# Retention with a snake feed-forward layer on one core: three q loads and two k loads by rows of eight tokens, decay tables by doubling on GpSimd, and another order of the first token group

## The chip, the cores and the metric

The kernel runs on one core of one Trainium2 chip. The metric is the device time of one execution in microseconds (us), the median of several runs. A core has TensorE (PE in the profile; PEld is its weight load), VectorE (DVE), ScalarE (ACT), GpSimd (POOL) and SyncE (SP), and 16 DMA engines.

## The reference, cut to what matters

```python
def _attn_ref(q, k, v):                      # q, k, v: (4, 8, 768, 64), float32
    gamma = 1.0 - 2.0 ** (-5.0 - np.arange(H))
    for t in range(S):
        state = gamma[None, :, None, None] * state + einsum('bhd,bhe->bhde', k[:, :, t], v[:, :, t])
        y[:, :, t] = D ** -0.5 * einsum('bhd,bhde->bhe', q[:, :, t], state)

def _moe_ref(x, w_in, w_out, alpha):         # x: (3072, 512), w_in: (512, 2048), w_out: (2048, 512)
    h = x @ w_in
    s = np.sin(alpha * h)
    return (h + s * s / (alpha + 1e-09)) @ w_out

x = attn.transpose(0, 2, 1, 3).reshape(B * S, H * D);  out = _moe_ref(x, ...)
```

Four sequences go through a retention layer with a decay gamma of its own for each of 8 heads; its result, per token the 8 heads side by side, goes through two matrix products with a snake function between them. The output is float32.

## The kernel before, in words

Each sequence of 768 tokens is cut into 6 chunks of 128 tokens, 24 in all. The list `order` puts the first chunk of each of the four sequences first (e0 to e3), then the other five of each; P[n] below is its n-th chunk. `sizes` makes ten groups of 4, 2, 2, 2, 2, 2, 2, 2, 2 and 4 chunks. A group passes the feed-forward layer together: a `Slot` takes one or more of 16 slices f of 128 hidden features. Its matmuls (L481) make `ph` in PSUM, ACT takes the sine (L484), ACT or DVE squares it (`sq("A")`, L489, or `sq("D")`, L491), and DVE's `add` (L496) writes `gT`. `ff_out` (L506) multiplies a slice of `gT` by `w_out` into `po`, for one chunk at a time. While a group's slots run, the `ff_out` of the group before fills TensorE between them, and the retention of the chunks of the next group is put in by a table (`where`, `atts`).

Retention of the first chunks needs no state: `half_T` transposes q (i=0) and k (i=1) on TensorE by an identity, `stage_A` (L276) makes the scores and has DVE multiply them by the decay matrix `dec` (L286), `stage_M` (L306) multiplies by v, and ACT copies the result to `xT`. For later chunks `burst` does it all: `inter` (q by the state `s_q`), `round_of` or `mix` (masked scores by v), `scores` of the next chunk, `sums` or `round_of` (k by v, for the state). A `nop` that waits for an earlier matmul (`behind`) stands in each burst. There the decay is taken by powers: v is scaled by `kg` or `kgq` (`scale_v`), the result by `qg[:, c]`, the table for chunk c of a sequence (`leave`, L433). `first_state` makes the state after e0; that after e1, e2 and e3 is made in the burst that ends the sequence before, from the raw k and v of those chunks.

Loads are issued on GpSimd, which casts float32 to bfloat16 on the way, one by one in the order of the program. A chunk load (`load_chunk`, L100) puts 128 tokens on 128 partitions, so its pieces are one head of one token: 1024 pieces of 256 B read and 128 B written for 128 KB. A half of a quarter of `w_in` (L131) is 512 pieces of 512 B written, a quarter of `w_out` (L135) 512 pieces of 1024 B, half of it 256. Only q and k of e0 come through SP, in float32 (`near`), and are cast on chip. The next 16 loads stand at the top; the other early ones are issued behind the front part of the program.

Ahead of the first feed-forward slot TensorE is kept busy with `idle_work(n)`: n matmuls of 512 columns on zeros. The tables for decay are made there too: `dec` by ACT from `tio` (the token index along the row), then multiplied by the mask on DVE (L563); `qg[:, 0]` by four Exps on ACT (`grow`, L554); `step` by five small Exps; `qg[:, c]` for c above 0 by one multiplication on GpSimd each (L229). `tok` is written by two iotas on GpSimd (L165). An Exp table and later a Sin table are loaded on ACT (L178, L588).

Group 0 (e0 to e3) is written out by hand (L657 to L708). Slices 0 to 3 are first computed for three chunks only (384 columns), while e3 is still on its way; then e3's 128 columns of the four slices in one Slot (`nf=4`, 16 matmuls), then slices 4 to 15 with 512 columns each. `F(ts, fs)` runs `ff_out` for several chunks. P[4], P[5] and P[6] are transposed (`stage_T`, L264) and the first two bursts run in its last third; `fill(n)` takes `ff_out` pieces of the third and fourth chunk.

PSUM buffers come by tags: "mm" has four of one bank, "two" and "pa" one of two banks each.

Of the kernel before, what the change touches and what calls it, by code (L numbers as in the profile page):

```python
# [16 lines left out]
def kernel(  # L17
# [32 lines left out]
    sizes = [4]+[2]*8+[4]  # L50
# [34 lines left out]

    def load_chunk(j, names="qkv"):
        for name, src in (("q", q), ("k", k), ("v", v)):
            if name not in names:
                continue
            if name == "v":  # L90
                t = big.tile([128, H, D], BF16, name="vr", tag="vr", bufs=11)
            else:
                if ("qk", j) not in raw:
                    raw["qk", j] = big.tile([128, 2, H, D], BF16, name="qkr", tag="qkr", bufs=9)
                t = raw["qk", j][:, "qk".index(name)]
# [61 lines left out]

    load_chunk(0, "v")
    load_chunk(order[1])
    load_chunk(order[2])  # L160
    for h in range(2):
        load_w_in(0, h)
    tok = consts.tile([128, NCH, 2], F32, name="tok")
    for b in range(2):
        nc.gpsimd.iota(tok[64 * b:64 * b + 64], pattern=[[C, NCH], [64, 2]], channel_multiplier=1, base=0,  # L165
                       allow_small_or_imprecise_dtypes=True)
    load_chunk(order[3], "qk")
    for h in range(2):
        load_w_out(0, h)
    load_chunk(order[3], "v")  # L170
    load_w_in(1)
    load_w_out(1)
# [7 lines left out]
    nc.vector.tensor_scalar(ident, tio, pos[:, 0:1], None, op0=ALU.is_equal)  # L180
    lg = consts.tile([128, H], F32, name="lg")
# [13 lines left out]
    lgp = consts.tile([128, NP], F32, name="lgp")  # L195
    for p in range(NP):
        for e in range(2):
            nc.vector.memset(lgp[64 * e:64 * e + 64, p:p + 1], lng[2 * p + e])
# [3 lines left out]
                         lg[:, None, :].to_broadcast([128, NCH, H]))  # L202
    kgq = consts.tile([128, NCH, H], F32, name="kgq")
# [3 lines left out]

    def later_tables():
# [15 lines left out]
    step = consts.tile([128, NCH, NP], F32, name="step")  # L224
    cscale = consts.tile([128, 1], F32, name="cscale")
    nc.vector.memset(cscale, lscale)

    def decay_table(c):
        nc.gpsimd.tensor_mul(qg[:, c], qg[:, 0], step[:, c, :, None].to_broadcast([128, NP, C]))  # L229
# [14 lines left out]
    def half_T(j, i, eng, bank=None):  # L244

        if i == 0:
            st["qkT", j] = work.tile([128, 2 * NP, 128], BF16, name="qkT", tag="qkT", bufs=6)
        pt = psum.tile([128, NP, 128], BF16, name="pt", tag="mm", bufs=4) if bank is None else bank.rearrange("i (p t) -> i p t", p=NP)
        for p in range(NP):
            nc.tensor.transpose(pt[:, p, :], raw["qk"[i], j][:, 2 * p:2 * p + 2, :].rearrange("p h d -> p (h d)"), ident)  # L250
        o = st["qkT", j][:, i * NP:(i + 1) * NP, :]
        if eng is nc.scalar:
# [23 lines left out]
    def stage_A(j):  # L276
        qkT = st["qkT", j]
        pa = psum.tile([128, 2, NP, 128], F32, name="pa", tag="pa")
        for p in range(NP):
# [4 lines left out]
        aT = work.tile([128, 2, NP, 128], BF16, name="aT", tag="aT", bufs=2)  # L284
# [525 lines left out]
```

## Time and profile before

| | |
|---|---|
| median of 3 runs | 210.59 us (210.5 to 211.37) |
| the profiled execution | 210.93 us, of which its span is 209.1 us and 1.8 us lie around it |
| PE busy | 199.3 us, 95% of the span |
| DVE, ACT busy | 151.9 us each, 73% |
| POOL busy | 116.5 us, 56% |
| granted TensorE clock | 1.00 |
| DMA | 24.76 MB in 102026 packets, 93024 of them under 512 B |
| chain that ended last | PE 77%, DMA 13%, POOL 6%, issue 2% |

The 16 DMA engines are busy nine tenths or more of each fortieth of the span until about 125 us. PE is busy nine tenths or more from the third fortieth on. Times below are counted from the start of the span. A row of the timeline gives the start, the length and the engine, the line, the operation and its tiles, the count, and in brackets what the engine sat idle for before it; matmuls are pipelined, so the distance between starts tells what a row of them costs, and the lengths overlap. DMA landings are read from the trace's record of each transfer's 16 engines; a transfer has landed when the last one reports.

### The profile page before, as it was taken

Reading aid. Unit: us, or ns where it says so; the run is one execution under the profiler, and the core shown is the slowest. Engines: PE = TensorE matmul, PEld = TensorE weight load, DVE = VectorE, ACT = ScalarE, POOL = GpSimd, SP = SyncE. Lnnn points to the kernel's source line nnn. Section 1 sums busy time; section 2 is a strip of 40 time slices with the busy share of each in tenths; the row PEclk is TensorE's granted clock in tenths of the full one; section 3 lists DMA queues with packets and bytes.
Section 4 is the critical chain, followed back from the end, with each engine's and each line's share of the span. In section 5 each row is a group of like instructions: output and inputs, shape, how many; then the busy total and the mean of one; then the engine's idle time right before and its main releaser. Section 6 shows DMA issues by size and latency. Waiting matters only on the chain.

```text
span 209.1 us, 5702 instructions
## 1 busy us (share of the span) xinstructions
PE 199.3 (95%) x2327; PEld 123.6 (59%) x2354; DVE 151.9 (73%) x310; ACT 151.9 (73%) x309; POOL 116.5 (56%) x157
## 2 busy tenths in 40 slices
PE   7898999999999999999999999999999999999994
PEld 2444544457776766766666766766767654444453
DVE  4788788877989968768868768867788965656220
ACT  7777687557998787787787787786785779999001
POOL 8999948599999999999599911002022200000000
PEclk9999999999999999999999999999999999999999
DMA  9999999999999999999999995412412101010212
GB/s 130 149 170 194 202 200 184 151 161 198 161 126 142 79 167 183 182 100 180 143 173 159 145 176 54 103 57 47 102 54 52 50 5 50 2 50 3 100 50 100
DMA packets 102026, 24.76 MB, mean 118 GB/s; under 512 B 93024, under 2 KB 99056, under 8 KB 102000
## 3 DMA queue, kind: packets, MB, share of 16 engines
q0 software_dynamic: 79248, 13.38, 87.9%
q1 hardware_dynamic: 22608, 10.96, 26.0%
q8 instruction: 18, 0.29, 0.6%
q14 instruction: 8, 0.07, 0.1%
q10 hardware_dynamic: 144, 0.07, 0.1%
HBM read 27.27 MB, written 6.29 MB: 160 GB/s over the span
## 4 chain that ended last, share of the span: by engine, by line
PE 77%; DMA 13%; POOL 6%; issue 2%; DVE 0%; POOLq 0%; DVEq 0%
PE po L506 34%; PE ph L481 33%; DMA qkr<-in_k_dram 5%; DMA w_out<-in_moe_w_out_dram 5%; DMA w_in<-in_moe_w_in_dram 3%; PE py L336 2%; POOL qg L229 2%; PE poh L531 2%; POOL qkr L100 2%; PE py L386 1%; POOL vr L100 1%; POOL w_in L131 1%; PE pa L346 1%; PE py L395 1%; PE pt L264 1%
## 5 line engine op out<-in xcount | busy, mean ns | idle before, releaser
L496 DVE SCALAR_TENSOR_TENSOR gT<-s,rec_alpha,ph 128x256 bf16<-128x256 f32 (+3 forms) x164 | 79.9, 523 | 32.8 <-ACT s L489 32.5
L481 PE MATMUL ph<-xT,w_in 128*128 128x256 bf16 (+3 forms) x652 | 98.1, 290 | 0.3
L484 ACT ACTIVATE s<-ph,alpha_sb 128x256 f32<-128x256 f32 (+3 forms) x164 | 76.2, 507 | 30.3 <-PE ph L481 30.2
L506 PE MATMUL po<-w_out,gT 128*128 128x512 bf16 x346 | 91.3, 379 | 3.1 <-issue 2.7
L481 PEld LDWEIGHTS <-w_in 128*128 128x128 bf16 x656 | 63.3, 98 | 33.8 <-issue 1.1
L489 ACT ACTIVATE s<-s 128x512 f32<-128x512 f32 (+1 forms) x91 | 57.0, 627 | 2.9
L506 PEld LDWEIGHTS <-gT 128*128 128x128 bf16 x368 | 33.9, 98 | 29.5
L452 POOL CAST s_q<-s_f 128x256 bf16<-128x256 f32 x5 | 2.0, 397 | 35.0 <-DVE s_f L448 18.0
L518 DVE COPY o_sb<-po 128x512 f32<-128x512 f32 x20 | 13.8, 691 | 9.8 <-PE po L506 9.8
L120 POOL DMA_DIRECT2D qk_seq<-in_q_dram x24 | 17.0, 766 | 2.7 <-DMA v_seq<-in_v_dram 2.6
L120 POOL DMA_DIRECT2D qk_seq<-in_k_dram x24 | 16.8, 716 | 0.8 <-issue 0.4
L120 POOL DMA_DIRECT2D v_seq<-in_v_dram x24 | 16.9, 765 | 0.0
L156 POOL TENSOR_TENSOR v_seq<-v_seq,kgq 128x512 bf16<-128x512 bf16 x13 | 13.5, 1057 | 4.6 <-DMA v_seq<-in_v_dram 4.6
L433 DVE TENSOR_TENSOR xT<-py,qg 128x512 bf16<-128x512 f32 x19 | 13.0, 685 | 0.8 <-PE py L402 0.8
L361 DVE TENSOR_TENSOR aTw<-pa,maskq 128x768 bf16<-128x768 f32 x13 | 12.4, 954 | 0.0
L100 POOL DMA_DIRECT2D vr<-in_v_dram x11 | 10.2, 927 | 1.2 <-DMA w_in<-in_moe_w_in_dram 1.1
L551 PE MATMUL spare<-warm 128*128 128x512 bf16 x24 | 8.4, 480 | 1.2 <-DVE warm L176 1.2
L535 ACT COPY o_sb<-poh 128x256 f32<-128x256 f32 (+1 forms) x2 | 0.6, 320 | 11.7 <-PE poh L531 11.2
L349 DVE TENSOR_TENSOR aT<-pa,mask 128x1024 bf16<-128x1024 f32 x7 | 8.5, 1218 | 0.0
L452 ACT CAST s_q<-s_f 128x256 bf16<-128x256 f32 x14 | 5.5, 393 | 3.1 <-DVE s_f L446 2.7
L100 POOL DMA_DIRECT2D qkr<-in_k_dram x7 | 6.3, 896 | 1.7 <-DMA w_out<-in_moe_w_out_dram 1.7
L100 POOL DMA_DIRECT2D qkr<-in_q_dram x7 | 6.4, 910 | 0.9 <-DMA w_in<-in_moe_w_in_dram 0.9
(99 smaller groups left out, 160.8 us busy)
## 6 DMA issues: line engine op xcount, KB each, us to landing
out_dram<-o_sb SPq DMA_DIRECT2D x23, 256.0 KB, 2.6
w_in<-in_moe_w_in_dram POOLq DMA_DIRECT2D x6, 256.0 KB, 10.3
w_out<-in_moe_w_out_dram POOLq DMA_DIRECT2D x3, 512.0 KB, 11.2
vr<-in_v_dram POOLq DMA_DIRECT2D x11, 128.0 KB, 5.5
qk_seq<-in_q_dram POOLq DMA_DIRECT2D x16, 80.0 KB, 7.1
qk_seq<-in_k_dram POOLq DMA_DIRECT2D x16, 80.0 KB, 5.2
v_seq<-in_v_dram POOLq DMA_DIRECT2D x16, 80.0 KB, 5.3
qkr<-in_q_dram POOLq DMA_DIRECT2D x7, 128.0 KB, 6.8
```

The source lines that it names most:

```text
L100: nc.gpsimd.dma_start(out=t, in_=chunk_of(src, j))
L120: nc.gpsimd.dma_start(out=o, in_=src[bt, head(b, m, e), cs[0] * C:, :].rearrange("(f i) d -> i f d", i=64))
L156: eng.tensor_mul(t, t, by[:, j % NCH, :, None].to_broadcast([128, H, D]))
L349: return {"mask": lambda: nc.vector.tensor_mul(aT.rearrange("p e n t -> p (e n) t"), pa.rearrange("p e (n t) -> p (e n) t", n=NP), mask_bc)}
L361: return {"mask": lambda: nc.vector.tensor_mul(aT, pa[:, :, 0:384].rearrange("p e (m t) -> p e m t", m=2), maskq[:, None, None, :].to_broa ...
L433: nc.vector.tensor_mul(o, st["pyw", old][:, :, 0:256].rearrange("p b (m t) -> p b m t", m=2), by)
L481: nc.tensor.matmul(self.ph[:, m, :], w_in[:, i, f * 128:(f + 1) * 128], xT[g][:, i, self.lo:self.hi], start=(m == 0 and i == 0), stop=(i = ...
L484: nc.scalar.activation(out=self.s[:, m, :], in_=self.ph[:, m, :], func=ACTF.Sin, scale=alpha_sb[:, f:f + 1])
L489: nc.scalar.activation(out=self.s, in_=self.s, func=ACTF.Square)
L496: nc.vector.scalar_tensor_tensor(gT[self.g][:, f, self.lo:self.hi], self.s[:, m, :], rec_alpha[:, f:f + 1], self.ph[:, m, :], op0=ALU.mult ...
L506: nc.tensor.matmul(po[g, ts], gT[g][:, f, ts * C:(ts + 1) * C], w_out[:, f, :], start=(f == 0), stop=(f == FF - 1))
L518: nc.vector.tensor_copy(o_sb, po[g, ts])
```

## The change

**Loads.** The q of e1, e2 and e3 and the k of e2 and e3 are read by `load_rows`: a partition holds eight consecutive tokens of one head, so a load has 128 pieces, each 2 KB read and 1 KB written. `half_T` then transposes 64 x 64 pieces, 16 for each half, and the copy out of PSUM puts the tokens in order. Heads 0 to 3 and 4 to 7 now lie on the two halves of the partitions for all first chunks, so `dec` is laid out by `h // NP`, and the halves that are read as before take 8 transposes instead of 4. Since k of e2 and e3 no longer has tokens on partitions, `back_k` transposes it back from `kT`, two halves each, in the bursts of P[10], P[11], P[15] and P[16]; `sums` takes half the tokens at a time. The order of the loads is another one.

**Tables.** The mask moves into the exponent: `far` is the token index plus 1e6 where the mask is zero, and `dec` is made from it; the multiplication on DVE goes. `qg[:, 0]` is built on GpSimd by seven doublings from powers `gp` that DVE makes by squaring, `qg[:, c]` from `qg[:, c - 1]`. `grow`, `step` and the iotas for `tok` go; `tok` is made by four small DVE operations. `later_mask` moves to the start of group 2.

**Order.** `stage_A` is split from its multiplication by `dec` (`mask_A`). Group 0 is written as another list of slots. In the bursts `sums` comes before `scores` where the state of another sequence is made, and the last burst does half of `mix` ahead of its `nop`.

```diff
+    def rows_of(t, j):
+        b, c = divmod(j, NCH)
+        return t[b, :, c * C:(c + 1) * C, :].rearrange("h (i f) d -> h i (f d)", f=8)
+    def load_rows(j, name):
+        src = q if name == "q" else k
+        t = raw[name, j] = big.tile([128, 8, D], BF16, name=f"{name}f", tag=f"{name}f", bufs=3 if name == "q" else 2)
+        nc.gpsimd.dma_start(out=t.rearrange("p f d -> p (f d)"), in_=rows_of(src, j))
+    def by_rows(j, name):
+        return name == "q" and j in order[1:4] or name == "k" and j in order[2:4]
...
-    load_chunk(0, "v"); load_chunk(order[1]); load_chunk(order[2]); w_in(0, 0), w_in(0, 1); [tok iotas]
-    load_chunk(order[3], "qk"); w_out(0, 0), w_out(0, 1); load_chunk(order[3], "v"); w_in(1); w_out(1)
+    q e1; q e2; k e1; k e2; q e3; v e0; v e1; w_in(0, 0); v e2; w_in(0, 1); k e3; v e3;
+    w_out(0, 0); w_out(0, 1); w_in(1); w_in(3, 0)
...
-    w_in(2, 0), w_in(2, 1); decay_table(1..4); w_out(2); w_in(3, 0), w_in(3, 1); qk P4; w_out(3); v P4; qkv P5; qkv P6
+    decay_table(0); w_out(1); w_in(2, 0), w_in(2, 1); w_in(3, 1); q P4; w_out(2); v P4; k P4; decay_table(1), (2);
+    q P5; decay_table(3); k P5; w_out(3); q P6; k P6; v P5; v P6; decay_table(4)
...
+    far = consts.tile([128, C], F32, name="far")
+    nc.vector.tensor_scalar(far, tio, pos[:, 0:1], 1e6, op0=ALU.is_lt, op1=ALU.mult)
+    nc.vector.tensor_add(far, far, tio)
...
-        nc.scalar.activation(out=dec[:, h % 2, h // 2, :], in_=tio, func=ACTF.Exp, scale=lng[h], bias=back[:, h:h + 1])
+        nc.scalar.activation(out=dec[:, h // NP, h % NP, :], in_=far, func=ACTF.Exp, scale=lng[h], bias=back[:, h:h + 1])
+    gp = consts.tile([128, 8, NP], F32, name="gp")
...
+    for n in range(7):
+        nc.vector.tensor_mul(gp[:, n + 1], gp[:, n], gp[:, n])
...
     def later_tables():
+        for b in range(2):
+            for f in range(2):
+                nc.vector.tensor_scalar_add(tok[64 * b:64 * b + 64, :, f], pos[64 * b:64 * b + 64], float(64 * (f - b)))
...
     def decay_table(c):
-        nc.gpsimd.tensor_mul(qg[:, c], qg[:, 0], step[:, c, :, None].to_broadcast([128, NP, C]))
+        if c:
+            nc.gpsimd.tensor_mul(qg[:, c], qg[:, c - 1], gp[:, 7, :, None].to_broadcast([128, NP, C]))
+            return
+        for n in range(7):
+            w = 1 << n
+            nc.gpsimd.tensor_mul(qg[:, 0, :, w:2 * w], qg[:, 0, :, 0:w], gp[:, n, :, None].to_broadcast([128, NP, w]))
...
+        if by_rows(j, "qk"[i]):
+            for f in range(8):
+                for x in range(2):
+                    nc.tensor.transpose(pt.rearrange("i p t -> i (p t)")[half(x), 64 * f:64 * f + 64],
+                                        raw["qk"[i], j][half(x), f, :], ident[half(x), half(x)])
+            o = o.rearrange("d m (i f) -> d m i f", f=8)
+            pt = pt.rearrange("d p t -> d (p t)").rearrange("d (f m i) -> d m i f", f=8, m=NP)
...
+    def back_k(j, x):
+        if x == 0:
+            raw["k", j] = big.tile([128, 2, NP, D], BF16, name="kn", tag="kf", bufs=2)
+        pt = psum.tile([128, NP, D], BF16, name="pt", tag="mm", bufs=4)
+        for m in range(NP):
+            for f in range(2):
+                nc.tensor.transpose(pt[half(f), m, :], st["kT", j][half(x), m, half(f)], ident[half(x), half(x)])
+        nc.vector.tensor_copy(raw["k", j][:, x], pt)
...
         if not wide(old):
             last = round_of(old, now, 0)
+        elif now is not None and now is not old:
+            last = sums(now, st["py", old], 256)
         more = scores(new) if new is not None else {}
+        if old in P[10:12] + P[15:17]:
+            back_k(e2 if old in P[10:12] else e3, (P.index(old) - 10) % 5)
...
+        if new is None:
+            mix(old, [(0, 0), (1, 1)])
+            rest = [(0, 1), (1, 0)]
         behind(last)
...
         def keep():
+            if wide(old) and now is not old:
+                [one copy of py[:, 256:384] and two additions of py[:, 384:512] into s_f]
```

The two rewritten lists of loads are shortened to names, `(i, h)` being the quarter and its half. The front now runs, on the engines' queues in this order: k cast of e0 on ACT; `idle_work(9)`; q cast of e0 on DVE, `later_tables`; `kg`; two idle; both halves of e0 (ACT, DVE copies) and q of e1 (DVE); alpha's transpose; `stage_A(e0)`; k of e1 (ACT); `kgq`, three idle; `mask_A(e0)`; q of e2 (ACT); `stage_A(e1)`; `stage_M(e0)`; k of e2 (ACT); `mask_A(e1)`; `stage_M(e1)`; `stage_A(e2)`; `mask_A(e2)`; q of e3 (DVE); the Sin table; `stage_M(e2)`; four idle. Then group 0, where `s3` is a slot of 384 columns, `t` the four slices of e3's columns, and `pairs(f)` is `ff_out` of slice f for chunks 0 and 1:

```
s3(0) s3(1) T(k e3) stage_A(e3) in between s3(2) s3(3); pairs 0; scale_v e1; pairs 1; scale_v e0; stage_M(e3);
ff_out(2, 1), (2, 2); pairs 2; t; slot 5; slot 4; ff_out(2, 3); pairs 3; slot 6; slot 7; ff_out(2, 4); pairs 4; slot 8; pairs 5;
first_state; slot 9; ff_out(2, 5); slot 10; slot 12; slot 11; pairs 6, 7, 8; T(P4) on ACT, slots 13, 14, 15 and pairs 9 to 14
between them; T(P5) on ACT; burst(P4); pairs 15; T(P6); burst(P5); 13 fills in all, as before
squares on DVE: slots 0, t, 5, 9, 11; on ACT: all others
```

More of the change, by code (lines that the diff above doesn't have):

```diff
@@ new lines @@
+    stage_A(e0)
+    half_T(e1, 1, nc.scalar)
+    idle_work(1)
+    nc.scalar.activation(out=kgq, in_=expoq, func=ACTF.Exp, scale=-1.0)
+    idle_work(2)
+    nc.scalar.copy(alpha_sb, pal)
+    mask_A(e0)
+    idle_work(1)
+    half_T(e2, 0, nc.scalar)
+    stage_A(e1)
+    stage_M(e0, front[:, 0])
+    half_T(e2, 1, nc.scalar)
+    idle_work(1)
+    mask_A(e1)
+    decay_table(0)
+    load_w_out(1)
+    load_w_in(2, 0)
+    load_w_in(2, 1)
+    load_w_in(3, 1)
+    load_chunk(order[4], "q")
+    load_w_out(2)
@@ new lines @@
+    load_chunk(order[4], "v")
+    load_chunk(order[4], "k")
+    decay_table(1)
+    decay_table(2)
+    load_chunk(order[5], "q")
+    decay_table(3)
+    load_chunk(order[5], "k")
+    load_w_out(3)
+    load_chunk(order[6], "q")
+    load_chunk(order[6], "k")
+    load_chunk(order[5], "v")
+    load_chunk(order[6], "v")
+    decay_table(4)
+    stage_M(e1, front[:, 0])
+    stage_A(e2)
+    idle_work(2)
+    mask_A(e2)
+    half_T(e3, 0, nc.vector)
+    idle_work(1)
+    nc.scalar.activation(out=tiny, in_=warm[:, 0:1], func=ACTF.Sin)
@@ L711 @@
+    pairs(6)
+    pairs(7)
+    pairs(8)
     load_chunk(P[7])
```

402 lines of the change are left out of this document (224 added, 178 removed).

## The prediction

> **What bounds the kernel now.** I read the chain of waits first, in order of time.
>
> ```profile
> 8.40 7.19 DMA w_in<-in_moe_w_in_dram
> ...
> 21.51 9.47 DMA w_out<-in_moe_w_out_dram
> 30.98 0.28 issue
> 31.26 9.52 DMA qkr<-in_k_dram
> 40.83 0.41 PE pt L264 x8
> ```
>
> Up to 40.8 us the chain runs through loads, behind that through TensorE alone. So a load that lands sooner can pay before 41 us, and every TensorE instruction added behind it costs its full time. The TensorE timeline of group 0 shows what the loads cost (start, length, work, idle time before):
>
> ```profile
> 14.75 1.46 PE L481 MATMUL ph<-xT,w_in 128*128 128x384 bf16 x8
> 16.48 0.40 PE L250 MATMUL fourth<-ident,qkr 128*128 128x128 bf16 x4 [0.28 <-DMA qkr<-in_q_dram]
> ...
> 20.73 0.41 PE L312 MATMUL pye<-aT,vr 128*64 128x128 bf16 x8 [0.57 <-DMA vr<-in_v_dram]
> ...
> 23.36 3.44 PE L481 MATMUL ph<-xT,w_in 128*128 128x512 bf16 x15
> ```
>
> Starts give the prices: a 512-column matmul 0.215, a slot of 384 columns 0.64, a full slot 0.86, 16 transposes of L264 0.57. By these, 14.75 to 16.48 holds 1.28 us of work and lost 0.45 (q of e3); 18.69 to 21.08 holds 1.42 and lost 0.97 (v of e3); 40.30 to 42.14 holds 1.42 and lost 0.42 (k of P5). Together 1.84. 35.41 to 37.38 holds 1.85 and lost 0.12 at P4's transposes. At 23.36 the next weights (w_in(1), landed 23.2) arrive as TensorE gets there.
>
> The GpSimd timeline prices the loads, the DVE timeline the front:
>
> ```profile
> 5.06 0.92 POOL L100 DMA_DIRECT2D qkr<-in_q_dram  x1
> 5.93 0.93 POOL L100 DMA_DIRECT2D qkr<-in_k_dram  x1
> ...
> 15.88 1.58 POOL L131 DMA_DIRECT2D w_in<-in_moe_w_in_dram  x2 [0.57 <-DMA w_in<-in_moe_w_in_dram]
> 17.53 4.04 POOL L229 TENSOR_TENSOR qg<-qg,step 128x512 f32<-128x512 f32 x4
> ```
>
> ```profile
> 4.07 0.43 DVE L559 CAST qb<-o_sb 128x512 bf16<-128x512 f32 x1 [0.57 <-DMA o_sb<-in_q_dram]
> ...
> 6.02 1.22 DVE L563 TENSOR_TENSOR dec<-dec,mask 128x1024 f32<-128x1024 f32 x1
> ```
>
> A chunk load takes 0.9 us to issue, and the 17th load waited for the 9th to land (15.59): eight are in flight at most.
>
> **The loads.** Back to back, chunk loads land 0.87 us apart (k of e3 17.28, q of e3 16.44, and 0.9 for the first six). w_out(2), 512 KB in pieces of 1 KB written, landed 31.0, 2.55 after the load before it: 0.64 for 128 KB. A row load has such pieces, so five save 5 x 0.23 = 1.15 us of DMA time. Bounds: the chunk loads' 0.87 (a rival, below), and the same 0.23 once more to the other side, 0.41; w_in's 512 B pieces (1.3 for 256 KB, 0.65 for 128) say that the curve is flat by then, so 0.64. Issue falls from 0.9 to about 0.7 (w_out halves of 256 pieces: 0.72), 1.0 us of GpSimd in all, and the iotas' 0.54 goes; neither is waited for.
>
> One thing has to be chosen. From first to last engine the first six loads land within 0.6 to 0.75 us; v of e2 within 1.4, w_in(0, 0) within 2.5, all later ones within about 2.2. If the same laggards remain, landings move by the 1.15 alone; if the spread stays at 0.7, by 1.5 more. I take 1.4, the value of the last chunk load, so 0.85 earlier.
>
> Then: v of e2 is now behind w_in(0, 0) and lands at 14.27 + 0.87 - 0.92 (four row loads) = 14.2, less 0.85 is 13.4, against 12.25. w_in(1) has the same fourteen loads ahead as before: 23.2 - 1.15 - 0.85 = 21.2. v of e3 and q of e3 land before 17, so their waits go. w_in(2, 0) now stands behind w_in(3, 0) (1.3 us by the halves' spacing): 27.1 + 1.3 - 2.0 = 26.4. k of P5 comes in time (its wait goes).
>
> **The front.** DVE gains two operations for `far` (0.25 each), seven dependent multiplications of 4 columns (0.06 by a memset to 0.48 by the dependent L187; I take expo's 0.2: 1.4) ahead of q's cast, which moves from 4.07 to about 6.0. Behind it four adds, eight memsets and a product, 1.4, ahead of the k copy. From 6.0: cast 0.43, tables 1.4, copies 0.42 and, read with a stride, up to 0.69 (L518's price for 512 unpacked columns), three masks of 1.22, and twice 0.5 since `pa` has one buffer and `stage_A` waits for the mask before. That ends at 13.6, beside v of e2 at 13.4 and 13.36 before; the 1.22 of L563 that goes ran from 6.02 to 7.24, ahead of a product that started at 7.51 only, so it pays nothing by itself. stage_M 0.35 and ACT's copy 0.58 give the first slot at 14.6 (14.75 before). The Sin table (1.28) now loads before that copy is due; before, it ended at 14.02 with the copy waiting. ACT loses 2.0 (`grow`) and 0.57 (`step`), off the path. GpSimd's doublings, 508 columns at 2 ns plus seven starts, are about 2 us (1.7 to 3.8) ahead of w_out(1): eight loads are queued then, over 6 us, so DMA does not run dry.
>
> From 14.6: four slots 2.56, k of e3 in 16 small transposes 0.3, stage_A 0.3, nine matmuls of `po` 1.92, stage_M 0.35, 16 matmuls for e3's slices 0.89. That ends at 20.9; slot 5 waits for w_in(1) to 21.2. Before, the same point is 23.36 less three matmuls already done, 22.7: 1.5 gained. Slot 8 would start at 27.51 - 1.5 = 26.0 but for w_in(2, 0) at 26.4: 1.1 kept. With k of P5, 0.42, and P4's 0.12 (its k lands at 34.2, TensorE comes at 34.4): **1.64** less at 47.6. The other small losses from 23.36 to 47.6, 1.0 in all by the same count, belong to the order of the slots; I leave them, and take half of them either way for the range.
>
> **What is added.** `back_k` is 8 transposes of 64 columns, four times. L264's 16 of 128 columns start 36 ns apart; half of that is 18, so 0.14 each, **0.57** in all. Bounds: 0.24 (L370's sixteen 64 x 64 matmuls all start within 0.12 us) and 1.15 (36 ns). [...]
>
> The four DVE copies (0.3) lie beside DVE's 32.5 us of waits for ACT at L496; uncovered, 1.2. `sums` by halves has twice the matmuls of half the depth, 0.12 (L370) against 0.24, twice: 0, at most 0.2. The two longer `keep`, 0.5 of DVE, end well ahead of the next burst, 7.8 us on. `later_mask`, 0.8 of DVE, has the same cover. The last burst fills its 0.16 of "issue" with half of `mix`: **-0.1**.
>
> Sum against the profiled 210.93: -1.64 + 0.57 - 0.1 = -1.17, so 209.76; the median lay 0.34 below that run: **209.4**. A measurement of this kernel tells 0.5% (1.05 us, here 209.54) from no change. Own range: spread 0.7 gives 0.65 more, small transposes 0.33, slot order 0.5 (207.9); spread 2.2 takes 0.85, `back_k` 0.58 (210.8).
>
> **Rivals.** *DMA order gives it back.* The engines lag as before, w_in(3, 0) ahead of its need holds w_in(2, 0) at 27.1 + 1.3 - 1.15 = 27.25, and slot 8 gains only 0.3; with 0.42 at P5, and 0.47 added: -0.25, so **210.3**. For it: w_in(3, 0) is needed only at slot 12, and DMA is saturated to 45 us. Against: nothing but the unknown spread.
>
> *Slower: ACT becomes the bound in group 0.* From 22 to 39.2 the windows give:
>
> ```profile
> 22.00:39.20 17.20, 17.09 (x109) 8.07 (x108) 14.10 (x25) 12.68 (x23) 10.77 (x14) 1.00 1.64 189
> ```
>
> ACT has 12.68 of 17.2 there. The change gives it nine squares of full slots instead of seven (2 x 0.63) and P4's copy (1.01): 14.95. If ACT keeps the 4.5 us in which it waits for `ph` (its order is fixed, and slots finish in bunches), the stretch takes 19.45, 2.25 longer. Banks of "mm" then come free late and TensorE stands. -1.5 at slot 5, +2.25, +0.47, and nothing at P5: +1.2, and **211.8**. It costs the whole gain from 1.0 us of stretch on, and shows as slower from 2.1. For it: ACT at 87%. Against: DVE loses two squares (1.4), and ACT's waits are slack wherever DMA sets the pace.
>
> *The loads do not get faster*: row pieces at the 0.87 of chunk loads, laggards as before. Then w_in(2, 0) lands at 27.1 + 1.3 = 28.4, 0.9 behind slot 8's old start; less 0.42 at P5, plus 0.47: 211.5. Against: w_out's pieces, alike in size, run at 0.64.
>
> **Chances.** Forecast 0.56 (0.47 faster by over 0.5%, 0.09 within: it lies just beyond the bound, but its low end reaches 1.5 us further, and most of what is near 210.3 is counted with the next case); DMA order 0.13 (0.01 faster, 0.10 within, 0.02 slower); ACT 0.25 (0.02 within, 0.23 slower); loads no faster 0.06 (0.02 within, 0.04 slower). Faster 0.48, same 0.23, slower 0.29. The range of 8 in 10 runs from 207.9, the forecast's low end, to 212.0, just over the ACT case.
>
> **What would show it.** Right: no DMA wait at q and v of e3 and at the transposes of P5; row loads landing about 0.64 apart; first L481 near 14.6, first 512-column slot near 21.2; the first slot of group 1 at 46.0 instead of 47.6; `back_k` four times under 0.2. Wrong: q's cast behind 7 us or a first slot behind 15.5 (DVE chain); TensorE waiting on ACT between 22 and 38, with ACT above 90%; w_in(2, 0) landing at 27 or later; bursts of P[10], P[11], P[15], P[16] longer by 0.4 or more.

## The result and the profile after

The changed kernel took **213.25 us** in the median of 20 runs (210.31 to 215.70) and the kernel before 210.34 (20 runs, 209.87 to 211.37); by these medians it is 2.9 us, or 1.4%, slower. The ratio of the fast runs alone, here the eleven up to 213.35, is 1.0066 with an interval of 1.0042 to 1.0091. The five runs at 215.2 and above have a mean granted clock of 0.99, and the profile was taken of such a run (215.70). The other fifteen stand in two bunches: four at 210.3 to 211.1 and eleven at 212.5 to 213.7, all at a clock of 0.998 or more. The kernel before has one bunch.

Three points cut a run into parts: the first slot of group 0, the first slot of group 1, and the end of the last matmuls. For the two profiled runs, in us:

| | first slot | to group 1 | to the end | total |
|---|---|---|---|---|
| before | 14.75 | 32.85 | 158.53 | 210.93 |
| after | 17.48 | 34.22 | 159.20 | 215.70 |
| difference | +2.73 | +1.37 | +0.67 | +4.77 |

**The front.** The chain of waits (start, length, what) now begins with k of e0, the load on SP, and goes on through TensorE, idle work included:

```profile
1.26 6.01 DMA o_sb<-in_k_dram
7.29 0.63 ACT kb L691
8.38 0.52 PE pr L291 x16
9.11 0.54 PE pa L341 x8
9.65 0.57 PE pt L298 x8
10.22 1.77 PE spare L636 x4
```

k of e0 landed at 7.27 us (its cast started at 5.32 before). The TensorE timeline has the pause, what four matmuls of idle work took behind it, and the first slot:

```profile
7.96 0.41 PE L298 MATMUL pt<-ident,kb 128*64 128x128 bf16 x8 [2.02 <-ACT kb L691]
...
10.15 1.84 PE L636 MATMUL spare<-warm 128*128 128x512 bf16 x4
...
16.61 1.04 PE L636 MATMUL spare<-warm 128*128 128x512 bf16 x4
17.48 0.81 PE L566 MATMUL ph<-xT,w_in 128*128 128x384 bf16 x4
```

The same four matmuls take 1.84 us at 10 us and 1.04 at 16.6. The page's row of the granted clock (tenths of full speed in 40 slices) has a dip there:

```profile
PEclk9789999999999999999999999999999999999999
```

From 8.40 to 11.81 us, 3.41 us long, the granted clock is 0.50, and 1.00 in the 3.4 us on either side. The fall came 0.44 us behind the end of the pause of 2.02 us.

**Group 0.** The DMA waits at q and v of e3 are gone, as forecast. In their place TensorE waits for DVE, twice within the first full slots:

```profile
28.05 0.82 PE L591 MATMUL po<-w_out,gT 128*128 128x512 bf16 x3 [1.68 <-DVE gT L581]
28.70 1.03 PE L566 MATMUL ph<-xT,w_in 128*128 128x512 bf16 x4
30.63 1.02 PE L566 MATMUL ph<-xT,w_in 128*128 128x512 bf16 x4 [0.90 <-DVE gT L581]
```

The DVE timeline shows four scalings of v in 4.71 us (singly 0.68, 0.68, 2.06 and 1.52), and squares (L576) of one shape at three lengths; the GpSimd timeline shows what ran beside them:

```profile
22.75 4.71 DVE L175 TENSOR_TENSOR vr<-vr,kg 128x512 bf16<-128x512 bf16 x4
27.91 1.50 DVE L576 TENSOR_TENSOR s<-s 128x512 f32<-128x512 f32 x1
31.15 0.68 DVE L576 TENSOR_TENSOR s<-s 128x512 f32<-128x512 f32 x1
35.94 1.96 DVE L576 TENSOR_TENSOR s<-s 128x512 f32<-128x512 f32 x1
```

```profile
24.41 2.51 POOL L258 TENSOR_TENSOR qg<-qg,gp 128x512 f32<-128x512 f32 x2
27.81 1.05 POOL L258 TENSOR_TENSOR qg<-qg,gp 128x512 f32<-128x512 f32 x1
35.30 1.05 POOL L258 TENSOR_TENSOR qg<-qg,gp 128x512 f32<-128x512 f32 x1
36.30 1.04 POOL L175 TENSOR_TENSOR vr<-vr,kg 128x512 bf16<-128x512 bf16 x1
```

The square at 31.15 had GpSimd's arithmetic to neither side and took 0.68, like the first two scalings, which ended before 24.41. The two long squares end at 29.41 and 37.90, each 0.55 to 0.56 us behind the end of a GpSimd product (28.86 and 37.34). In the window from 22 to 39.2 us (length, busy time of PE, PEld, DVE, ACT, POOL, then clock, DMA share, GB/s) DVE is at 16.17 of 17.2 and TensorE has lost 2.6 of its 17.09:

```profile
22.00:39.20 17.20, 14.49 (x92) 6.93 (x91) 16.17 (x22) 11.64 (x22) 15.16 (x17) 1.00 1.67 187
```

**The rest.** From the start of one burst to the next, three of the four bursts with `back_k` take 7.89 us instead of 7.76 and the fourth 7.93 instead of 7.91: 0.41 in all. The two that end a sequence, with `sums` ahead of `scores`, take 7.98 instead of 8.06, 0.16 less together. In group 2 TensorE waits at a slot for the eviction of `po` (0.28 for DVE at L603), and a step that took 1.74 takes 2.18: 0.44.

### The profile page after: what moved, and what is told of

The parts are those of the page before. It is cut to its first block, busy times and chain, and to the rows that moved or that the text cites. A ratio compares the mean times of both kernels' runs of the same rounds, so it can differ in the third digit from the quotient of the medians.

```text
span 213.9 us, 5978 instructions
## 1 busy us (share of the span) xinstructions
PE 204.3 (95%) x2473; PEld 125.0 (58%) x2473; DVE 157.0 (73%) x326; ACT 151.4 (71%) x304; POOL 117.5 (55%) x162
## 4 chain that ended last, share of the span: by engine, by line
PE 83%; DVE 8%; DMA 3%; ACT 3%; issue 1%; SPq 0%; ACTq 0%
PE po L591 35%; PE ph L566 34%; DVE gT L581 3%; DMA o_sb<-in_k_dram 3%; DVE vr L175 3%; PE py L404 2%; PE spare L636 2%; PE poh L616 2%; PE py L458 1%; ACT s L569 1%; PE pt L311 1%; DVE aT L353 1%; PE pa L414 1%; PE pa L421 1%; PE py L467 1%
## 5 line engine op out<-in xcount | busy, mean ns | idle before, releaser
L591 PE MATMUL po<-w_out,gT 128*128 128x512 bf16 x368 | 94.7, 380 | 1.7 <-DVE gT L581 1.7
L603 DVE COPY o_sb<-po 128x512 f32<-128x512 f32 x20 | 13.8, 690 | 9.9 <-PE po L591 9.8
L636 PE MATMUL spare<-warm 128*128 128x512 bf16 x24 | 8.9, 513 | 1.2 <-DVE warm L196 1.2
L353 DVE TENSOR_TENSOR aT<-pa,dec 128x1024 bf16<-128x1024 f32 x4 | 4.9, 1224 | 2.8 <-PE pa L341 2.7
L175 DVE TENSOR_TENSOR vr<-vr,kg 128x512 bf16<-128x512 bf16 x6 | 6.9, 1186 | 0.0
L576 DVE TENSOR_TENSOR s<-s 128x512 f32<-128x512 f32 (+1 forms) x5 | 5.4, 1078 | 1.9 <-ACT s L569 1.9
```

The lines of the kernel that those rows point to most:

```text
L175: eng.tensor_mul(t, t, by[:, j % NCH, :, None].to_broadcast([128, H, D]))
L591: nc.tensor.matmul(po[g, ts], gT[g][:, f, ts * C:(ts + 1) * C], w_out[:, f, :], start=(f == 0), stop=(f == FF - 1))
L603: nc.vector.tensor_copy(o_sb, po[g, ts])
L636: nc.tensor.matmul(spare["ps"], warm[:, :128], warm, start=True, stop=True)
```

## The experiments

All runs in one table: median in us (range, number of runs), ratio to the kernel before beside it (median 210.40 to 210.66) with its interval, taken as above, and from the profile the start of k's cast, the first slot, the stretch to group 1 and the rest.

| kernel | median | ratio | k cast | first slot | to group 1 | rest |
|---|---|---|---|---|---|---|
| e1_after | 213.63 (210.9-299.5, 11) | 1.0093 [1.0055, 1.0130] | 6.48 | 15.63 | 33.92 | 159.3 |
| e2_v0_first | 215.45 (214.1-216.0, 6) | 1.0229 [1.0199, 1.0259] | 5.37 | 17.62 | 34.07 | 159.4 |
| e3_tables_early | 212.97 (211.8-214.3, 6) | 1.0118 [1.0081, 1.0155] | 5.55 | 15.69 | 33.87 | 159.3 |
| e4_both | 212.44 (212.0-215.0, 6) | 1.0121 [1.0072, 1.0169] | 5.43 | 17.02 | 31.80 | 159.0 |
| e5_no_rows | 218.36 (214.9-218.7, 4) | | 5.20 | 19.16 | 32.33 | 158.3 |
| e6_tables_wout | 211.83 (210.9-213.9, 6) | 1.0064 [1.0026, 1.0102] | 6.92 | 16.99 | 31.16 | 158.9 |
| e7_before_pieces | 215.46 (1) | | 5.71 | 18.83 | 33.29 | 158.5 |
| e8_fix | 212.30 (211.8-213.7, 6) | 1.0089 [1.0059, 1.0120] | 6.01 | 17.47 | 32.68 | 158.7 |
| e9_no_rows | 211.03 (210.3-214.2, 12) | 1.0024 [0.9997, 1.0050] | 5.51 | 15.58 | 31.49 | 158.3 |
| e10_filler | 213.94 (211.0-214.3, 6) | 1.0104 [1.0051, 1.0158] | 6.84 | 15.65 | 34.27 | 159.4 |
| e11_tables_filler | 212.01 (211.1-213.5, 12) | 1.0061 [1.0036, 1.0086] | 5.67 | 15.67 | 32.08 | 158.8 |
| e12_no_rows_tables | 212.95 (212.2-213.2, 6) | 1.0100 [1.0069, 1.0131] | 5.28 | 15.37 | 33.56 | 158.7 |
| e13_short_front | 212.10 (211.9-213.1, 6) | 1.0087 [1.0060, 1.0114] | 5.57 | 15.88 | 32.84 | 159.3 |
| e14_no_rows_short | 212.83 (210.8-215.9, 12) | 1.0076 [1.0037, 1.0115] | 6.26 | 15.71 | 33.98 | 158.3 |
| e15_no_rows_clear | 211.24 (210.9-211.6, 12) | 1.0034 [1.0017, 1.0051] | 5.22 | 15.33 | 32.42 | 158.7 |
| e16_rows_clear | 210.88 (210.4-212.6, 12) | 1.0021 [0.9994, 1.0049] | 6.73 | 15.92 | 31.85 | 159.2 |

Front, stretch and rest are of the one profiled run and need not be the median's.

**e1: the changed kernel again, and e2: the loads that the front needs first.**

> The changed kernel again, unedited, to have several executions and a profile of an undisturbed one. Theory A (the k of e0, which comes through SP, shares the 16 DMA engines with row loads whose 1 KB pieces hold an engine for 0.1 us each, and so lands late): every execution shows the cast of k on ACT later than the 5.3 us of before, by an amount that varies from run to run, and the time varies with it, 210 to 216 us. Theory B (group 0's own order and DVE sharing with GpSimd cost it, whatever the front does): the distance from the first L566 to the first slot of group 1 is longer than the 32.9 us of before by 1 to 1.5 us in the quick executions too.

The second profile had no half clock: the first slot is at 15.63, and the idle work at 9.1 takes 1.04. So some 1.9 us of the front come from the pause and the clock, and 0.9 remain. Theory B holds beside it: with the front undisturbed, the stretch to group 1 is still 33.92, 1.1 us longer than before. (One of its eleven runs took 299 us at a clock of 0.66.)

```diff
-    q e1; q e2; k e1; k e2; q e3; v e0; ...
+    v e0; k e1; q e1; q e2; k e2; q e3; ...
```

> Only the order of the first seven loads is changed: v of e0 and k of e1, chunk loads with 128 B pieces, go first, then the row loads. Theory A: k of e0 lands near 5.3 us as before, the first slot starts at about 15.5 instead of 17.5, the spread of the times falls below 1 us, and the median falls to about 211. Rival (the k of e0 is late because more loads start earlier, whatever their pieces): k of e0 still lands at 6.5 to 7.3 and the time stays.

k of e0 came in time (cast at 5.37), but q of e1 then landed at 8.40, TensorE stood still for it instead, and the clock fell again, in all six runs (0.992):

```profile
8.44 0.44 PE L291 MATMUL pr<-ident,qf 64*64 64x64 bf16 x16 [1.91 <-DMA qf<-in_q_dram]
...
9.97 1.89 PE L636 MATMUL spare<-warm 128*128 128x512 bf16 x4
```

The late transfer was only exchanged for another, and the forecast of 211 was missed; the pause is what costs.

**e3: the decay tables in one go, and e4: e2 and e3 together.**

```diff
-    decay_table(0)
+    for c in range(5):
+        decay_table(c)
     load_w_out(1)
...
-    decay_table(1); decay_table(2); [behind k P4]   decay_table(3); [behind q P5]   decay_table(4) [behind v P6]
```

> Only GpSimd's four products for the decay tables of chunks 1 to 4 are moved: right behind the doublings, where they run from about 16.4 to 20, instead of among the loads at 24 to 29 and 35. Theory B (DVE's two-operand products on bfloat16 and its squares run at half speed or less while GpSimd multiplies): the four scalings of v take 0.7 us each instead of 1.2, the square of slot 5 and slot 9 0.7 instead of 1.5 and 2.0, TensorE's waits for gT (1.7 and 0.9 us) shrink, and the time falls by 1 to 2 us. Rival (GpSimd is no cause; DVE's order is): durations fall but TensorE's waits stay, time the same within 0.5 us; later issue of w_out(1) costs nothing by the eight loads in flight.

> The edits of the two runs before together: v of e0 and k of e1 first, tables right behind the doublings. If both theories hold the gains add, 3 to 4 us below the changed kernel's median, 209 to 210; if one cost hides the other, the sum is no better than the better of the two.

In e3 every square of 512 columns took 0.69 and the four scalings 2.49, so DVE was slow for GpSimd's sake. The median fell by only 0.7, not by 1 to 2: GpSimd, busy with tables, issued w_out(1) and w_in(2, 0) later, and TensorE waited for those:

```profile
28.29 0.81 PE L591 MATMUL po<-w_out,gT 128*128 128x512 bf16 x3 [1.30 <-DMA w_out<-in_moe_w_out_dram]
29.64 1.04 PE L566 MATMUL ph<-xT,w_in 128*128 128x512 bf16 x4 [0.54 <-DMA w_in<-in_moe_w_in_dram]
```

e4 started 1.3 us later (half clock as in e2, behind a wait of 1.40 for q of e1), met none of these waits over 0.16, and took 31.80; its median is 212.44, where 209 to 210 was forecast.

**e6: e3 with another sixteenth load; e8: e6 with the front's loads first and `later_mask` early.**

```diff
     load_w_in(1)
-    load_w_in(3, 0)
+    load_w_out(1)
...                                  [w_in(3, 0) now behind w_in(2, 1)]
```

```diff
-    q e1; q e2; k e1; k e2; q e3; v e0; v e1; w_in(0, 0); v e2; ...
+    v e0; k e1; q e1; q e2; k e2; v e1; v e2; w_in(0, 0); q e3; ...
...
     stage_A(e0)
+    mask_A(e0)
+    half_T(e1, 0, nc.vector)
...
+    later_mask()                     [behind rec_alpha, no longer in group 2]
```

> Tables of chunks 1 to 4 right behind the doublings, and w_out(1) in the place of w_in(3, 0), which follows w_in(2, 1); loads at the front as changed. Theory B: squares on DVE 0.69, the waits for w_out(1) and w_in(2, 0) that the move alone brought (1.30 and 0.54 us) go, first L566 to the first slot of group 1 takes 31.5 to 32 us instead of 33.9, and the median falls by 1.5 to 2 us to about 211.5. Rival (DVE's order, not GpSimd): 33 or more.

> The changed kernel with all that the runs point to: v of e0 and k of e1 ahead of the row loads, v of e1 and e2 ahead of w_in(0, 0); q of e1 transposed behind the scores of e0, so that its landing holds nothing up; tables right behind the doublings, w_out(1) ahead of w_in(3, 0); the second mask at the front again, where DVE waits. If the three causes (late k of e0, GpSimd beside DVE, the mask in group 2) are all there is: first slot at 14 to 14.8, 31.8 from there to group 1, 158.9 behind it, 208.5 to 209.5 in all, faster than both kernels. If the front has another bound (the chain of masks on DVE): first slot at 15.5, 210.5.

e6 has group 0 as it was forecast: 31.16 us and no wait of TensorE above 0.16. Its profile again has a half clock in the front (mean 0.992), behind a pause of 1.24. e8 gained nothing, 212.30 where 208.5 to 209.5 was forecast: q of e1 came at 8.74, TensorE paused three times (0.39, 0.52 and 0.61), and the clock fell (mean 0.992). Its `later_mask`, now beside the tables on GpSimd, took 1.93 and 1.04 us instead of 0.77 and 0.28 in the changed kernel, and a square beside GpSimd's scaling of v 1.89.

**e5 and e9: no row reads.**

```diff
     def by_rows(j, name):
-        return name == "q" and j in order[1:4] or name == "k" and j in order[2:4]
+        return False
...
-        if old in P[10:12] + P[15:17]:
-            back_k(e2 if old in P[10:12] else e3, (P.index(old) - 10) % 5)
```

> The changed kernel with none of the five row loads: q and k of e1 to e3 as chunk loads in the same places of the order, no back_k. Theory A (the 1 KB pieces are what holds up k of e0): k of e0 lands at 5.3 us as before, the times spread by less than 1.5 us; DMA landings from w_in(0, 0) on are 1.0 to 1.2 us later than with row loads; `back_k`'s 0.5 us goes. Median 211.5 to 212.5, below the changed kernel: the row loads lose more at the front than they save. Rival (more loads started early, whatever their pieces): k of e0 stays at 6.4 to 7.3.

e5 is inconclusive: with the rows gone q of e1 shared a tile with k of e1, and k's load waited for it (TensorE stood still for 3.29 us). e9 gives each its own.

> The changed kernel with the five row reads replaced by loads in the form of the kernel before (q and k of e1, e2, e3 token by token, back_k left out, each load with a tile of its own this time); the doublings, later_mask and the other order of group 0 stay. Theory A (1 KB pieces of the row reads hold up k of e0 on the other queue): k of e0 lands at 5.2 to 5.7 us instead of 7.3, TensorE's wait for it shrinks to under 0.6 us, the granted clock stays at 1.0, the first slot starts at 14.5 to 15.3, and with bursts of 7.77 us in phases P10 to P12 and P15 to P17 the end of the matmuls after group 1's first slot is 158.4 to 158.7: median 210.0 to 211.5, of which group 0's own stretch (32.5 to 34) is the larger part. Rival (the order of the loads alone holds k back, rows or not): k of e0 at 6.5 us or later, the first slot at 16 or later, median 212.5 or more.

k of e0 landed at 5.49 and the clock held (1.0), as the theory has it, but the first slot is at 15.58, no earlier than in e1. TensorE now waits for k of e1 (0.73) and for v of e0 (0.66), which in the new order is the sixth load and lands at 10.92 (6.23 before). The median is 2.2 us below the changed kernel's.

**e7: the kernel before, with two loads of 1 KB pieces first.**

```diff
+    for h in range(2):
+        load_w_out(0, h)
     load_chunk(0, "v")
```

> The kernel before, with the two halves of w_out(0) (pieces of 1 KB written, as in a row load) moved to the head of GpSimd's loads, ahead of v of e0. Theory A: k of e0, on SP's queue, lands at 6 to 7.5 us instead of 5.3, with a few last pieces trickling in, though nothing of the change is in this kernel. Rival (the cause is something else in the change): 5.3. The time itself says little, since all chunk loads come 2.6 us of DMA later: 212 to 214.

k of e0 landed at 5.68 instead of 5.30 and alpha at 6.71 instead of 5.89. So 1 KB pieces on the other queue do hold SP's transfers back, by some 0.4 to 0.8 in this one run, less than in the changed kernel; the other loads were two places later, so its total says nothing.

**e10: idle work in the pause, and e11: the same in e6.**

```diff
     half_T(e0, 0, nc.scalar)
+    idle_work(5)
     half_T(e0, 1, nc.vector)
```

> The changed kernel with five more matmuls of idle work (about 1.3 us) on TensorE between the transposes of q of e0 and those of k of e0, where it stood still for 2.02 us in the profile of the changed kernel. Theory (the pause lets the granted clock fall to half, and that costs up to 2 us on top of the late landing): no halved clock in the profile, first slot at 15.4 to 16.2 us, the rest as in the changed kernel (34 us to group 1, 159.2 to the end): median 212 to 213, the runs within 2.5 us of each other instead of 5.4. Rival (the clock falls for another reason than the pause): a halved window between 8 and 13 us again, first slot at 17 or later, runs spread over 5 us.

> The changed kernel with all five decay tables ahead of the later loads, the load of w_out(1) in place of the sixteenth, and the same five matmuls of idle work. Theory (two causes that add up: pause and clock in the front, DVE beside GpSimd in group 0): first slot at 15.4 to 16.2, 31.2 us from there to group 1, 158.9 to the end, 4.75 of start and finish: 210.3 to 211.0, so the kernel before's time within 0.4 per cent. Rival (the two repairs don't add up, since the earlier start only runs into later loads of weights): the stretch from the first slot to group 1 grows to 32.5 or more, median 211.8 or more.

In e10 TensorE's wait shrank from 2.02 to 0.43 us, no run had a mean clock below 0.999, and the first slot is at 15.65: the clock was the pause's doing. k of e0 had still landed late, at 6.82, so the landing by itself costs next to nothing (e3, with 5.52, starts at 15.69). Yet the median stayed, since five of six runs were in the upper of the two bunches. e11 has no slow square and 32.08 us to group 1 in its profiled run (211.28); its median, 212.01, missed the forecast of 210.3 to 211.0, and what its slower runs do isn't shown.

**e12: e9 with e6's tables and w_out(1)** (the edits of both, above).

> The two repairs of tables and w_out(1) together with token-by-token loads in place of the five row reads (no back_k); powers by doubling, later_mask and group 0's order stay. Theory (rows cost the front its start and 0.5 us of bursts, tables on GpSimd in group 0 cost DVE its speed; the other order of group 0 is a gain by itself): first slot 14.6 to 15.3, 31.2 to 31.8 to group 1, 158.3 to 158.6 to the end, 4.75 around them: median 208.9 to 210.3, faster than before by 0.2 to 0.7 per cent. Rival (without the row reads' 1.15 us of DMA time the weights come late for the new order of group 0): waits for w_in(1) or w_in(2,0) of 0.5 us or more, 33 us to group 1, median 211 or more.

The rival: w_out(2) landed at 35.37 and TensorE waited 1.07 us for it; the scalings met the tables, now at the front of the group (3.53 instead of 2.49).

**e13 and e14: less idle work ahead of the first slot, in e11 and in e9.**

```diff
     stage_A(e2)
-    idle_work(2)
...
-    idle_work(1); idle_work(1)       [on either side of the Sin table]
     stage_M(e2, front[:, 0])
-    idle_work(4)
```

> The kernel with early tables, early w_out(1) and five matmuls of idle work in k's wait, with eight others taken out behind the third chunk's A (2+1+1 beside its mask, 4 between its M and the first slot). In that kernel's profile the mask ends at 14.31 us, M starts at 14.45 and ends at 14.8, and the four matmuls (1.04 us) stand between it and the first slot at 15.67. Theory (the front now ends with idle work, not with a wait, and the row reads' earlier landing of w_in(0,0) at 12.4 lay unused): first slot at 14.7 to 15.0; of that 0.7 to 1.0 us reach group 1, since w_in(2,0) has landed by 25.7: 32.1 to 32.5 us from the first slot to group 1, median 210.9 to 211.4 instead of 212.0. Rival (the slots only run into the loads): 33 us from the first slot to group 1, waits on w_in of 0.5 us or more, median unchanged at 211.8 to 212.3.

> The kernel without row reads (token by token, later_mask, doublings and the other order of group 0 kept), with the same eight matmuls of idle work taken out ahead of the first slot. Theory: first slot at 14.6 to 14.9 instead of 15.58, of which 0.5 to 1.0 us reach group 1; median 210.0 to 210.5, faster than the kernel before by 0.1 to 0.3 per cent. Rival (an earlier start puts the DVE's squares back beside GpSimd's tables at 24.8 to 28.9): squares of 1.5 us or more in the profile, 32.5 to 34 us from the first slot to group 1, median 211 or more.

The theory that idle work lay on the path fell. Without it e13 waits in its place, for the mask and then for ACT's copy of the third chunk. From the end of the mask to the slot it takes 1.22 us instead of e11's 1.36, and the slot starts no sooner:

```profile
14.80 0.41 PE L379 MATMUL front<-aT,vr 128*64 128x128 bf16 x8 [1.05 <-DVE aT L353]
15.88 1.46 PE L566 MATMUL ph<-xT,w_in 128*128 128x384 bf16 x8 [0.67 <-ACT xT L382]
```

To group 1 e13 takes 32.84, with a wait of 1.26 for w_out(2). And the half clock came back with the idle work gone: 3 of the 6 runs of e13 and 6 of the 12 of e14 have a mean clock of 0.992 or less, none of the 24 of e11 and e9.

e14 told more than was asked. Its profiled run, at full clock, starts 0.13 us later than e9 and takes 2.5 us more from there to group 1. First e9's, then e14's DVE and GpSimd timelines:

```profile
23.94 0.69 DVE L574 TENSOR_TENSOR s<-s 128x512 f32<-128x512 f32 x1
24.77 2.17 POOL L258 TENSOR_TENSOR qg<-qg,gp 128x512 f32<-128x512 f32 x2
```

```profile
24.06 2.27 DVE L574 TENSOR_TENSOR s<-s 128x512 f32<-128x512 f32 x1
24.72 2.51 POOL L258 TENSOR_TENSOR qg<-qg,gp 128x512 f32<-128x512 f32 x2
```

In e9 the square ends at 24.63, before GpSimd multiplies; in e14 it would have ended at 24.75, after 24.72, and takes 1.58 us more. The next square then meets the third table (1.68). In these two runs a tenth of a microsecond in the front decides which of the two happens (210.28 against 212.83 us in all). That the two bunches of the changed kernel come of the same is likely, but no run of its lower bunch was profiled.

**e15 and e16: the tables moved to where DVE squares nothing**, in e9 and in e10.

```diff
     load_chunk(order[4], "k")
-    decay_table(1); decay_table(2)
     load_chunk(order[5], "q")
-    decay_table(3)
     load_chunk(order[5], "k")
+    decay_table(1); decay_table(2)
     ...
     load_chunk(order[6], "v")
+    decay_table(3)
     decay_table(4)
```

> The kernel without row reads (its idle work kept), with decay tables 1 and 2 moved behind the loads of q and k of P5 and tables 3 and 4 behind those of v of P5 and P6, so that GpSimd multiplies at about 28.4 to 30.5 and 35.6 to 37.7 us, while the DVE squares at 23.9, 26.5, 31.2 and 34.5. Theory (a square that meets a GpSimd multiplication takes 1.5 to 2.3 us instead of 0.69, and a tenth of a microsecond decides whether it does): all squares at 0.7 us in the profile, 31.3 to 31.8 us from the first slot to group 1, median 210.2 to 210.7 instead of 211.03, the runs within 2 us of each other instead of 3.9. Rival (the spread has other roots, the landing of k of e0 and the clock): median 210.9 to 211.3 and the same spread.

> The changed kernel with five matmuls of idle work in k's wait (213.94 median), with the decay tables moved in the same way. Theory: squares at 0.7 us, 31.3 to 32 us from the first slot (15.65) to group 1 instead of 34.3, 158.9 to the end: median 210.9 to 211.7, so 2 us or more off the kernel with the filler alone, and what is left above the kernel before is the front's 0.9 us and the bursts' 0.5. Rival (the slow squares only took slack): 33 us or more to group 1, median 213 or more.

e16's median is 3.1 us below e10's (2.8, each against the kernel before beside it) with nothing but the place of three GpSimd instructions among the loads; the loads of P5, which they now follow, land no earlier (q at 36.03 against 35.88). It is 2.4 below the changed kernel's. Its squares, and the window from 22 to 39.2 us:

```profile
24.30 0.69 DVE L576 TENSOR_TENSOR s<-s 128x512 f32<-128x512 f32 x1
...
26.89 0.68 DVE L576 TENSOR_TENSOR s<-s 128x512 f32<-128x512 f32 x1
...
31.52 0.68 DVE L576 TENSOR_TENSOR s<-s 128x512 f32<-128x512 f32 x1
...
34.70 0.69 DVE L576 TENSOR_TENSOR s<-s 128x512 f32<-128x512 f32 x1 [1.05 <-ACT s L569]
```

```profile
22.00:39.20 17.20, 16.99 (x137) 8.45 (x138) 13.79 (x24) 14.69 (x27) 13.38 (x15) 1.00 1.68 187
```

TensorE is back at 16.99 us. e15's runs lie within 0.74 us, against 3.9 of e9, which fits the squares as a cause of the spread. They are not the only one: e16's runs still spread over 2.2 us, six at 210.4 to 210.6 and six at 211.2 to 212.6, and its profile, without a slow square, is of the upper six (211.77). e15's median is not lower than e9's, nor the 210.2 to 210.7 forecast; in its profile w_in(1) landed at 23.12 and TensorE waited for loads (0.34, 0.44 and 0.22). No kernel here beats the kernel before; e16 and e9 can't be told from it.

## Why the prediction was wrong

It forecast 209.4 us, 14.6 for the first slot, 31.4 from there to group 1 and 0.47 more behind. At 213.25 it was 3.85 off, and outside its range: a gain was forecast, and a loss came. Two steps failed. In the front, the working followed DVE alone: it left out what stands ahead of each step on TensorE, and the transfer of k of e0, behind whose pause the clock fell to 0.50 for 3.41 us. In group 0, the decay tables' new place among DVE's products was put at nothing, and cost 2 to 3 us.

- **The first slot at 14.6** failed, in two ways. At full clock it is 15.6 to 15.9 with row reads. The powers took 1.34 (1.4), the strided copy 0.69 (0.69). But q's cast came at 5.0, not at 6.0 (DVE's idle 0.57 ahead of it before was not counted as cover), and DVE then stood idle for the transposes of k of e0, 1.35 us in e11. So the first mask was not held by the DVE chain; that it starts at 8.98 in e11, where the working gives 8.94, is luck. The two gaps between the masks, costed at 0.5 each for `pa`'s one buffer, were 0.71 and 0.93: ahead of `stage_A` on TensorE stand the transposes of q of e2 in the first and `stage_M(e1)` in the second. And from the end of the third mask (14.31) to the slot it took 1.36 instead of 0.93. Together 1.07. The second way was left out altogether: the time of k of e0. It landed at 5.3 before and between 5.5 and 7.3 in eight profiles with row reads in the new order, 5.2 to 6.2 in five without. The pause and the half clock cost up to 1.9 more, in a quarter of the runs; where the clock held, the landing cost next to nothing (15.63 in e1 with 6.46, 15.69 in e3 with 5.52).
- **Group 0, 31.4 from the first slot to group 1**, was right where DVE runs undisturbed: 31.16, 31.85 and 32.08 in e6, e16 and e11, and 31.49 in e9, where one square of 0.95 is the only slow one. The waits for e3's loads and for P4 and P5 did go. The working failed where it costed the tables' new place at GpSimd's time alone. It didn't ask what two-operand products DVE runs beside them: 2 to 3 us in the four profiles that have row reads and the tables in that place (33.9 to 34.3 to group 1), and, by e10 and e16, the term behind most of the loss in the median. The kernel before had shown it: a scaling of v at 20.99 us, beside the last of the four products at 17.53 to 21.57, took 1.12 instead of 0.69.
- **The loads.** w_in(1) was forecast at 21.2 and landed at 21.4 to 22.1 in the eleven profiles with row reads, mean 21.75; in four without (e9, e12, e14, e15), 22.0 to 23.1, mean 22.4. So the rows save about 0.6 (0.4 without e15's 23.1), not 1.15; the direction was right, and "no faster" fell. From first to last engine the loads around w_in(1) still land over 2.0 us, so the choice of 1.4 was wrong. w_in(2, 0) came at 27.1 (26.4 forecast), with no wait of note: the DMA order rival didn't decide.
- **ACT becomes the bound in group 0** fell. Its busy time in the stretch was forecast at 14.95 and is 14.69 in e16, with TensorE at 16.99: its waits were slack. The rival's 211.8 was near for another reason; DVE, of which the text said that it loses two squares, was the bound, not by count but by length.
- **`back_k` 0.57**: 0.41 measured; eight small transposes start within 0.10 us, first to last.
- **The last burst -0.1 and `later_mask` 0.** From the start of the last burst to the next slot it takes 1.54 us (1.55 before): nothing was gained. The idle time named "issue" goes with a matmul missing from the trace, not with time: such rows have three matmuls and span what four take (168.74 to 169.61 us in the kernel before). `later_mask` had less cover than was taken. It stands in DVE's queue of group 2 ahead of the copy of `po` that TensorE waits for. Where DVE spends up to 1.72 us on it and on the next scaling of v together, nothing is lost (e5, e9, e11, e14), nor in e8, which makes the mask at the front; in the other eleven profiles of the new order the two take 1.75 to 2.38 us and the burst interval grows by 0.12 to 0.66, with row reads or without (e12, e15). What lengthens the two there wasn't tried: GpSimd only issues loads beside them.

For the run of e10 (214.12) the sum closes: +0.90 in the front, +1.42 to group 1, +0.88 behind are 3.20 above the 210.93 of before; the forecast had -0.15, -1.45 and +0.47. For e16 (211.77): +1.17, -1.00 and +0.68.

## What to carry to other kernels

When a step moves to GpSimd, or moves in GpSimd's order, list the two-operand SBUF products that DVE runs in that stretch, and put GpSimd's arithmetic where there are none (here squares of 0.69 us took up to 2.27 beside it); where runs fall into two bunches, look for such a collision at the edge. Fill a pause of TensorE ahead of a dense part with idle work: in the changed kernel's profile the pause cost again through the clock (the first slot at 17.48 us, in e10, with five matmuls in the pause, at 15.65). When the order of loads changes, follow the transfer on the other queue too, and the last operand of each step, not only the weights.

## What the hardware showed that was not expected

- A DVE product of two SBUF operands beside a GpSimd product was, in these traces, not slowed by a share but held up. Squares of 0.69 us took 0.95 to 2.27, scalings of 0.68 up to 2.06, and the thirteen lengthened squares of 128x512 in the changed kernel, e1, e8, e9, e10 and e14 all end 0.55 to 0.56 us behind the end of a GpSimd product, whenever they began, as if DVE did its work when GpSimd was through. GpSimd lost time in turn: in the changed kernel its second product, beside the end of a scaling, took 1.38 instead of 1.05, and in e14 the pair 2.51 instead of e9's 2.17. Products with one operand in PSUM kept their time (three of L579 in 2.07, beside a GpSimd product in e9 and without one in e14). `later_mask`, with one tensor operand in SBUF, was held up too (1.93 and 1.04 in e8, 0.77 and 0.28 in the changed kernel). The traces don't show who goes first: e14's square starts 0.66 us ahead of GpSimd's product by the records, and it is the square that grew by 1.58, GpSimd's pair by 0.34; in e15 a scaling that starts 0.10 ahead keeps its 0.68, and GpSimd's product takes 1.48. Nor do the traces show what in the two engines does it. Spans on GpSimd are rough.
- The half clock came at places that differ between runs: from 8.40 to 11.81 us in the changed kernel's trace, 3.41 us. The other profiled runs that show one have a mean clock of 0.992 (e2, e4, e6, e7, e8) and 0.984 (e5), which is what one and two such stretches take off (half of 3.41 us in 212 is 0.8%). It came behind single pauses of 1.24 (e6) to 3.29 us (e5), in e8 behind three of 0.39 to 0.61, and not behind one of 1.27 (e1). So here the length of the pause doesn't decide it, and neither does TensorE's busy time in the 3.41 us before: 2.17 us in e6 (5.82 to 9.23) led to a half clock, 1.75 in the changed kernel's group 0 (25.46 to 28.88, with the wait of 1.68 for DVE) did not. What differs is the work: in the front mostly transposes and 64x64 pieces, in group 0 matmuls that fill the array. Counted as columns times the filled share of 128x128, the 3.41 us ahead of the changed kernel's fall (4.98 to 8.40) hold 2144 columns, and the least that a later stretch of that length holds there at full clock, up to 209.8 us, is 3584 (25.46 to 28.87). In e4, an estimate from its timeline, 2600 to 3100 stand ahead of the fall at about 10.0. That is a reading of these traces after the fact; no run tried it.
